# Decoding float64 weights with integer operations in a fused attention and two-FFN kernel

## The chip, the cores and the metric

The kernel runs on one core of one Trainium2 chip. The metric is the device time in microseconds (us) of one execution; the median of 3 runs of the kernel before is 885.85 us (885.5 to 887.36). A core has five engines with queues of their own: PE multiplies matrices, DVE, ACT and POOL work on elements, SP issues the DMAs.

## The reference

Windowed causal attention (4 batches, 8 heads, 576 positions, head size 64) gives 2304 tokens of 512 features. A first feed-forward block (512 to 1024 to 512, softmax gate and layer norm) and a second one (512 to 1536 to 512, SiLU gate) follow:

```python
def _attn_ref(q, k, v):
    scores = scale * np.matmul(q, k.transpose(0, 1, 3, 2))
    scores = np.where(mask, scores + bias[None], -1000000000.0)
    scores = scores - np.max(scores, axis=-1, keepdims=True)
    attn = np.exp(scores)
    attn = attn / (np.sum(attn, axis=-1, keepdims=True) + 1e-09)
    return np.matmul(attn, v).astype(np.float32)

def _moe_ref(x, w_in, w_out, g_ln):
    h = x @ w_in
    e = np.exp(h - np.max(h, axis=-1, keepdims=True))
    solu = h * (e / (np.sum(e, axis=-1, keepdims=True) + 1e-09))
    mu = np.mean(solu, axis=-1, keepdims=True)
    var = np.mean((solu - mu) ** 2, axis=-1, keepdims=True)
    return ((solu - mu) / np.sqrt(var + 1e-06) * g_ln @ w_out).astype(np.float32)

def _moe2_ref(x, w_gate, w_val, w_out):
    g = x @ w_gate
    return (g * (1.0 / (1.0 + np.exp(-g))) * (x @ w_val) @ w_out).astype(np.float32)
```

The five weight matrices arrive as float64. [...]

## The kernel before

The order of all instructions is made when the kernel is built. Generators describe the tasks, and an `Emitter` (its `run`, line 158) plays them against a model of engine times (`t_act`, `t_dve`, `t_pool`) and hands out instructions by a rank; where a step has several possible engines it takes the one that ends first by the model plus a handicap (1.6 us for DVE, 0.7 us for ACT). On the chip every engine then works through its own queue in that fixed order and waits on semaphores.

There are 20 attention steps (`score` and `attend`, lines 314 and 353: scores on PE, line 339; bias and row maximum on DVE, line 372; exponential on ACT, line 375; sum and reciprocal on DVE, lines 381 and 382; normalising on POOL, ACT or DVE, lines 387 and 389; transposes on PE, line 409; values on PE, line 441). Behind them come 18 token tiles of the first block (`up`, line 527; `flip`, line 589; `down1`, line 618), whose results go to DRAM (`yscr`) and come back (`load_y`, line 716). When attention has ended, its memory is given to the second block (`second_region`, line 666), which goes through 12 column chunks of the second weights, two to a pass (`load_w2`, line 701; `gate_val`, line 740; `down`, line 777). All large matrix products are in `pieces`, line 523. Each float32 operand is split into a rounded part (`high`, lines 202 and 203, on ACT or DVE) and a remainder (`low`, lines 206 and 208, on DVE or POOL), and three products are summed.

`decode` (line 213) makes one 128x512 block of weights, 52 times: 8 blocks of `w_in`, 8 of `w_out`, 36 of the second weights. A 512 KB DMA brings the pairs of words into tile `dw` (2 buffers). `lw` and `hw` are the low and the high words, every other element of `dw`. Before the change:

- line 225, ACT: `b` is the square of the high word read as float32.
- line 230, DVE: `a` is the high word, or zero where the square is under a limit.
- line 232, DVE: `b` is `a` shifted left by 3, masked. Line 234, DVE: the sign is put in from `a`.
- line 236, DVE: `a` is the exponent of `b`. Line 238, DVE: `a` becomes the low word scaled by that exponent. Buffer `dw` is given back here (line 240).
- line 241, POOL (or line 242, DVE): `b` is `b` plus `a` in float32.
- for `w_out` a scale on ACT or DVE (line 245), then `high` and `low`. `da` and `db` have 2 buffers each; `da` is held to the addition, `db` to the end of `low`.

All DMAs go through the one SP queue (line 193), in the order of the plan.

Of the kernel before, what the change touches and what calls it, by code (L numbers as in the profile page):

```python
# [8 lines left out]
F32 = mybir.dt.float32  # L9
F32R = mybir.dt.float32r  # L10
U32 = mybir.dt.uint32
AF = mybir.ActivationFunctionType
ALU = mybir.AluOpType
AX = mybir.AxisListType
# [7 lines left out]
P = 128  # L22
# [28 lines left out]
MIN_HIGH = 2.0 ** -15 * 1.125  # L51
# [123 lines left out]
def attention_then_two_ffns(ctx: ExitStack, tc: tile.TileContext, qk, v, w_in, w_out, g_ln, w2, ident_d, bias_d, out):  # L175


    nc = tc.nc
    em = Emitter()
    PE, DVE, ACT, POOL, DMA = "PE", "DVE", "ACT", "POOL", "DMA"  # L180
    yscr = nc.dram_tensor("yscr", [NT // 256, P, KM, 256], F32).ap()

    def t_act(n, sbuf=True, table=False):
        return (94 if sbuf else 51) + 94 * table + 0.833 * n

    def t_dve(n, fast=False):
        return 68 + (0.52 if fast else 1.042) * n

    def t_pool(n):
        return 149 + 2.104 * n  # L190

    def dma(dst, src, nbytes, deps=()):
        return (DMA, nbytes / 360.0, lambda: nc.sync.dma_start(dst, src), deps, 2000.0)

    const = ctx.enter_context(tc.tile_pool(name="const", bufs=1))
    dec = ctx.enter_context(tc.tile_pool(name="dec", bufs=1))
# [4 lines left out]
    def high(hi, src, n, sbuf=True):  # L201
        return [(ACT, t_act(n, sbuf), lambda: nc.scalar.copy(hi, src)),  # L202
                (DVE, t_dve(n, sbuf), lambda: nc.vector.tensor_copy(hi, src))]

    def low(lo, src, hi, n, sbuf=True):
        ways = [(DVE, t_dve(n), lambda: nc.vector.tensor_sub(lo, src, hi.bitcast(F32)))]
        if sbuf:
            ways.append((POOL, t_pool(n), lambda: nc.gpsimd.tensor_sub(lo, src, hi.bitcast(F32))))  # L208
        return ways

    dw_s, da_s, db_s = Slots(NDW), Slots(2), Slots(2)

    def decode(hi, lo, src, scale=None):


        yield dw_s
        words = dec.tile([P, 512, 2], U32, tag="dw", bufs=NDW, name="dw")
        got = yield dma(words, src.bitcast(U32), 524288)
        lw, hw = words[:, :, 0], words[:, :, 1]
        hf = hw.bitcast(F32)  # L220
        yield got
        yield db_s
        b = dec.tile([P, 512], U32, tag="db", bufs=2, name="db")
        bf = b.bitcast(F32)
        x = yield (ACT, t_act(512), lambda: nc.scalar.activation(bf, hf, AF.Square))  # L225
        yield x
        yield da_s
        a = dec.tile([P, 512], U32, tag="da", bufs=2, name="da")
        af = a.bitcast(F32)
        x = yield (DVE, t_dve(512), lambda: nc.vector.scalar_tensor_tensor(  # L230
            af, bf, MIN_HIGH * MIN_HIGH, hf, ALU.is_ge, ALU.mult), [x])
        x = yield (DVE, t_dve(512, True), lambda: nc.vector.tensor_scalar(  # L232
            b, a, 3, 0x3FFFFFF8, ALU.logical_shift_left, ALU.bitwise_and), [x])
        x = yield (DVE, t_dve(512), lambda: nc.vector.scalar_tensor_tensor(  # L234
            b, a, 0xC0000000, b, ALU.bitwise_and, ALU.bitwise_or), [x])
        x = yield (DVE, t_dve(512, True), lambda: nc.vector.tensor_scalar(  # L236
            a, b, 0xFF800000, None, ALU.bitwise_and), [x])
        x = yield (DVE, t_dve(512), lambda: nc.vector.scalar_tensor_tensor(  # L238
            af, lw, 2.0 ** -52, af, ALU.mult, ALU.mult), [x])
        em.give(dw_s, x)  # L240
        x = yield ([(POOL, t_pool(512), lambda: nc.gpsimd.tensor_add(bf, bf, af)),  # L241
                    (DVE, t_dve(512), lambda: nc.vector.tensor_add(bf, bf, af))], [x])
        em.give(da_s, x)
        if scale is not None:
            x = yield ([(ACT, 93 + t_act(512), lambda: nc.scalar.activation(bf, bf, AF.Copy, scale=scale)),
                        (DVE, 456, lambda: nc.vector.tensor_scalar_mul(bf, bf, scale))], [x])
        x = yield (high(hi, bf, 512), [x])
        x = yield (low(lo, bf, hi, 512), [x])
        em.give(db_s, x)
        yield x  # L250
# [102 lines left out]
    def attend(u):  # L353
# [17 lines left out]
        for j in range(2):  # L371
# [3 lines left out]
            ex.append((yield (ACT, t_act(cols, True, True), lambda j=j: nc.scalar.activation(  # L375
                e[0:n, j, 0:cols], e[0:n, j, 0:cols], AF.Exp, bias=st[0:n, j:j + 1], scale=-1.0,
                accum_out=st[0:n, 2 + j:3 + j]), [d])))
# [6 lines left out]
        def normalize(eng):  # L384
            if eng is nc.scalar:
                for j in range(2):
                    nc.scalar.activation(e[0:n, j, 0:cols], e[0:n, j, 0:cols], AF.Copy, scale=st[0:n, 6 + j:7 + j])
            else:
# [97 lines left out]
    def load_in():  # L486
        for half in range(2):
            cs = slice(half * 512, half * 512 + 512)
            for r in range(KM):
                def one(half=half, r=r, cs=cs):  # L490
                    yield from decode(win[0][:, r, cs], win[1][:, r, cs], w_in[r * P:(r + 1) * P, cs])
                d = em.start(one(), PW_IN + 0.01 * (half * KM + r))
                chain(d, win_ok[half][r])

    def load_out():
        for r in range(KF1):
            def one(r=r):
                if r == 0:
                    gln_ok.append((yield dma(gln, g_ln, 4096)))
                yield gln_ok[0]  # L500
                yield from decode(wout[0][:, r, :], wout[1][:, r, :], w_out[r * P:(r + 1) * P, :], gln[:, r:r + 1])
            d = em.start(one(), PW_OUT + 0.05 * r)
            chain(d, wout_ok[r])
# [23 lines left out]
    def up(i):  # L527
# [28 lines left out]
        for q, (a, a2) in enumerate(((sm, su), (sm2, su2))):  # L556
            y = yield (ACT, t_act(512, False, True), lambda q=q, a=a: nc.scalar.activation(
                e[:, q], h[q], AF.Exp, bias=mx, accum_out=a), [x])
            us.append((yield (DVE, t_dve(512), lambda q=q, a2=a2: nc.vector.scalar_tensor_tensor(
# [4 lines left out]
        for q, a in enumerate((va, va2)):  # L564
            vs.append((yield (ACT, t_act(512, True, True), lambda q=q, a=a: nc.scalar.activation(
                h[q], e[:, q], AF.Square, bias=nmu32, scale=1.0 / 32, accum_out=a), [x])))

# [133 lines left out]
    def load_w2(c):  # L701
        yield w2_s
        wp = pools["w2p"]
        t = [wp.tile([P, DF2], F32R, tag=f"w2{a}", bufs=NW2, name=f"w2{a}") for a in range(2)]
        wc[c] = t
        for j in range(3):
            cs = slice(j * 512, (j + 1) * 512)
            yield from decode(t[0][:, cs], t[1][:, cs], w2[c, :, cs])
            x = yield (POOL, 0.0, lambda: None)
            yield x  # L710
            w2_ok[c][j].settle(x.time)
# [144 lines left out]
```

## Time and profile before

| | us |
|---|---|
| median of 3 runs | 885.85 |
| the profiled execution | 887.44 |
| its span | 885.7 |
| PE busy | 825.1 (93%) |
| DVE busy | 492.9 (56%) |
| ACT busy | 372.8 (42%) |
| POOL busy | 317.0 (36%) |

The profile is of one execution, of 887.44 us, 1.6 us above the median; 1.74 us of it lie outside the span. PE is the busiest engine, but it isn't full everywhere: in the first sixth of the span and in a stretch around 380 us the other engines are fuller and PE idles. An average over the whole span hides that, so the views are read by stretches. The clock column is the clock that PE was granted, as a share of its upper level.

### The profile page before, as it was taken

How to read it: one execution, taken by the hardware profiler on the slowest of the kernel's cores; microseconds unless marked ns; L12 is line 12 of the kernel's file. 1: busy time of each engine (PE TensorE's matmuls, PEld its weight loads, DVE VectorE, ACT ScalarE, POOL GpSimd, SP SyncE). 2: the span in 40 equal slices, each digit the busy share in tenths (PEclk: the TensorE clock that was granted, in tenths of full speed). 3: DMA queues.
4: the chain of work that ended last, by engine and by line, in shares of the span. 5: the costliest groups of instructions: out<-in, count | busy, mean ns of one | idle time of the engine just before them, and what ended most of it. 6: DMA issues, size and time to landing. Idle time of an engine off the chain costs nothing.

```text
span 885.7 us, 13165 instructions
## 1 busy us (share of the span) xinstructions
PE 825.1 (93%) x4968; PEld 677.9 (77%) x4968; DVE 492.9 (56%) x1188; ACT 372.8 (42%) x948; POOL 317.0 (36%) x274
## 2 busy tenths in 40 slices
PE   5769879999999999968799999999999999999997
PEld 3547658788888888968588888887887887888885
DVE  5988993654556445888510186258337526822222
ACT  4667885864766656444432322122122213211110
POOL 2464661322123121665731154145216414521111
PEclk9779899999999999979999999999999999999999
DMA  7543311311121102333320022012003101100112
GB/s 253 168 138 105 96 60 44 107 37 54 50 72 49 36 8 97 119 104 112 120 94 1 1 72 72 1 49 72 24 0 86 58 1 48 47 1 13 60 57 85
DMA packets 23776, 59.12 MB, mean 67 GB/s; under 512 B 2592, under 2 KB 5280, under 8 KB 23712
## 3 DMA queue, kind: packets, MB, share of 16 engines
q1 hardware_dynamic: 23712, 58.28, 20.3%
q8 instruction: 39, 0.64, 0.3%
q14 instruction: 25, 0.20, 0.1%
HBM read 48.83 MB, written 9.44 MB: 66 GB/s over the span
## 4 chain that ended last, share of the span: by engine, by line
PE 70%; DVE 17%; POOL 4%; issue 4%; ACT 4%; DMA 1%; SPq 0%; POOLq 0%; ACTq 0%; DVEq 0%
PE gv L523 28%; PE bank L523 16%; PE o L523 15%; PE bank L441 3%; PE bank L409 3%; PE bank L339 3%; DVE db L234 2%; DVE da L230 2%; DVE da L238 2%; DVE da L236 2%; POOL db L241 2%; DVE e L372 2%; DVE db L232 1%; PE bank L605 1%; ACT e L375 1%
## 5 line engine op out<-in xcount | busy, mean ns | idle before, releaser
L523 PE MATMUL gv<-y,w 128*128 128x512 f32 (+1 forms) x1392 | 316.2, 378 | 3.1 <-POOL y L208 3.1
L523 PEld LDWEIGHTS gv<-y,w 128*128 128x128 f32 x1392 | 249.0, 189 | 57.6 <-POOL y L208 3.5
L523 PE MATMUL o<-w,a 128*128 128x512 f32 x648 | 170.0, 398 | 5.2 <-ACT ys L202 2.2
L208 POOL TENSOR_TENSOR a<-sg,a 128x512 fp32r<-128x512 f32 (+1 forms) x60 | 73.9, 1232 | 237.7 <-ACT a L202 237.2
L523 PEld LDWEIGHTS o<-w,a 128*128 128x128 f32 x648 | 121.1, 190 | 34.6 <-POOL a L208 3.8
L795 DVE TENSOR_TENSOR acc<-acc,o 128x512 f32<-128x512 f32 x90 | 61.2, 684 | 119.9 <-PE o L523 119.8
L523 PE MATMUL bank<-lnT,wout 128*128 128x256 f32 x864 | 116.9, 287 | 3.0 <-ACT lnT L202 2.5
L523 PEld LDWEIGHTS bank<-lnT,wout 128*128 128x128 f32 x864 | 109.0, 191 | 8.6 <-ACT lnT L202 2.7
L523 PE MATMUL bank<-win,xs 128*128 128x512 f32 x432 | 114.9, 404 | 0.1
L202 ACT CAST a<-sg 128x512 fp32r<-128x512 f32 (+1 forms) x59 | 34.0, 577 | 181.8 <-DVE sg L769 181.8
L769 DVE TENSOR_TENSOR sg<-sg,gv 128x512 f32<-128x512 f32 (+1 forms) x58 | 37.1, 639 | 126.7 <-PE gv L523 97.2
L241 POOL TENSOR_TENSOR db<-db,da 128x512 f32<-128x512 f32 x51 | 72.0, 1413 | 96.5 <-DVE da L238 93.9
L523 PEld LDWEIGHTS bank<-win,xs 128*128 128x128 f32 x432 | 76.5, 189 | 17.1 <-issue 2.1
L389 POOL TENSOR_TENSOR e<-e,st 128x512 f32<-128x512 f32 (+2 forms) x55 | 52.2, 948 | 103.9 <-DVE st L382 41.6
L375 ACT ACTIVATE e<-e,st 128x256 f32<-128x256 f32 (+2 forms) x160 | 75.0, 471 | 28.9 <-DVE st L372 28.8
L409 PE MATMUL bank<-ident,e 128*128 128x128 f32 (+2 forms) x288 | 47.7, 292 | 24.3 <-POOL e L389 15.0
L372 DVE CUSTOM_DVE_ANT_0 e<-bank,bias 128x256 f32<-128x256 f32 (+2 forms) x160 | 54.3, 376 | 17.2 <-PE bank L339 11.7
L409 PEld LDWEIGHTS bank<-ident,e 128*128 128x128 f32 (+2 forms) x288 | 31.4, 147 | 36.3 <-POOL e L389 18.2
L441 PE MATMUL bank<-pt,v 128*64 128x128 f32 (+2 forms) x576 | 51.4, 292 | 6.2 <-ACT pt L415 5.3
L230 DVE SCALAR_TENSOR_TENSOR da<-db,dw 128x512 f32<-128x512 f32 x52 | 46.6, 897 | 18.5 <-ACT db L225 18.4
L767 ACT ACTIVATE sg<-gv 128x512 f32<-128x512 f32 (+1 forms) x58 | 32.3, 557 | 56.3 <-PE gv L523 43.5
L202 ACT CAST w<-db 128x512 fp32r<-128x512 f32 x35 | 21.7, 621 | 80.1 <-POOL db L241 80.0
(70 smaller groups left out, 906.3 us busy)
## 6 DMA issues: line engine op xcount, KB each, us to landing
dw<-w SPq DMA_DIRECT2D x36, 512.0 KB, 3.6
raw<-qk SPq DMA_DIRECT2D x38, 256.0 KB, 3.7
yscr<-ys SPq DMA_DIRECT2D x9, 512.0 KB, 2.9
ysg<-yscr SPq DMA_DIRECT2D x9, 512.0 KB, 3.3
out<-acc SPq DMA_DIRECT2D x18, 256.0 KB, 2.0
v<-v SPq DMA_DIRECT2D x16, 256.0 KB, 2.8
dw<-w_in SPq DMA_DIRECT2D x8, 512.0 KB, 4.0
dw<-w_out SPq DMA_DIRECT2D x8, 512.0 KB, 3.5
```

The source lines that it names most:

```text
L202: return [(ACT, t_act(n, sbuf), lambda: nc.scalar.copy(hi, src)), (DVE, t_dve(n, sbuf), lambda: nc.vector.tensor_copy(hi, src))]
L208: ways.append((POOL, t_pool(n), lambda: nc.gpsimd.tensor_sub(lo, src, hi.bitcast(F32))))
L230: x = yield (DVE, t_dve(512), lambda: nc.vector.scalar_tensor_tensor(af, bf, MIN_HIGH * MIN_HIGH, hf, ALU.is_ge, ALU.mult), [x])
L241: x = yield ([(POOL, t_pool(512), lambda: nc.gpsimd.tensor_add(bf, bf, af)), (DVE, t_dve(512), lambda: nc.vector.tensor_add(bf, bf, af))], ...
L372: d = yield (DVE, t_dve(cols), lambda j=j: nc.vector.tensor_tensor_reduce(e[0:n, j, 0:cols], sc[0:n, j * 256:j * 256 + cols], bias[0:n, 2 ...
L375: ex.append((yield (ACT, t_act(cols, True, True), lambda j=j: nc.scalar.activation(e[0:n, j, 0:cols], e[0:n, j, 0:cols], AF.Exp, bias=st[0 ...
L389: eng.tensor_tensor(e[0:n, :, 0:cols], e[0:n, :, 0:cols], st[0:n, 6:8].unsqueeze(2).to_broadcast([n, 2, cols]), ALU.mult)
L409: nc.tensor.transpose(tp[0:kp, kb, j, 0:n], e[0:n, j, x * P:x * P + kp], ident[0:n, 0:n])
L441: nc.tensor.matmul(px[j * 64:(j + 1) * 64, pr, 0:n], vt[c - 1 + kb][0:kp, h * 64:(h + 1) * 64], pt[0:kp, kb, j, 0:n], start=(kb == 1), sto ...
L523: nc.tensor.matmul(o, terms[m][0], terms[m][1], start=(m == 0), stop=(m == len(terms) - 1))
L769: x = yield (DVE, t_dve(n), lambda: nc.vector.tensor_mul(sg, sg, gv[1][0]), [x, gv[1][1]])
L795: y = yield (DVE, t_dve(512), lambda o=o, tt=tt: nc.vector.tensor_add(acc[tt], acc[tt], o), [x])
```

## The change

`decode` is rewritten. The low word is read by ACT, scaled by 2^-29 and written as an int32 into `a` (a rounded 0 to 8). ACT takes the absolute value of the high word instead of its square. DVE clamps it from below, shifts it left by 3 with a mask, and puts in the sign bits straight from the high word in `dw`. `dw` is given back after that third DVE operation. POOL then adds `a` to the bit pattern of `b` as int32; the choice of DVE for this addition is gone. What follows (scale, `high`, `low`) stays. `a` is now taken before `b`.

```diff
     def decode(hi, lo, src, scale=None):
         yield dw_s
         words = dec.tile([P, 512, 2], U32, tag="dw", bufs=NDW, name="dw")
         got = yield dma(words, src.bitcast(U32), 524288)
         lw, hw = words[:, :, 0], words[:, :, 1]
         hf = hw.bitcast(F32)
         yield got
+        yield da_s
+        a = dec.tile([P, 512], U32, tag="da", bufs=2, name="da")
+        r = yield (ACT, t_act(512), lambda: nc.scalar.activation(a.bitcast(I32), lw, AF.Copy, scale=2.0 ** -29))
         yield db_s
         b = dec.tile([P, 512], U32, tag="db", bufs=2, name="db")
         bf = b.bitcast(F32)
-        x = yield (ACT, t_act(512), lambda: nc.scalar.activation(bf, hf, AF.Square))
-        yield x
-        yield da_s
-        a = dec.tile([P, 512], U32, tag="da", bufs=2, name="da")
-        af = a.bitcast(F32)
+        x = yield (ACT, t_act(512), lambda: nc.scalar.activation(bf, hf, AF.Abs))
+        x = yield (DVE, t_dve(512, True), lambda: nc.vector.tensor_scalar_max(bf, bf, MIN_HIGH), [x])
+        x = yield (DVE, t_dve(512, True), lambda: nc.vector.tensor_scalar(
+            b, b, 3, 0x3FFFFFF8, ALU.logical_shift_left, ALU.bitwise_and), [x])
         x = yield (DVE, t_dve(512), lambda: nc.vector.scalar_tensor_tensor(
-            af, bf, MIN_HIGH * MIN_HIGH, hf, ALU.is_ge, ALU.mult), [x])
-        x = yield (DVE, t_dve(512, True), lambda: nc.vector.tensor_scalar(
-            b, a, 3, 0x3FFFFFF8, ALU.logical_shift_left, ALU.bitwise_and), [x])
-        x = yield (DVE, t_dve(512), lambda: nc.vector.scalar_tensor_tensor(
-            b, a, 0xC0000000, b, ALU.bitwise_and, ALU.bitwise_or), [x])
-        x = yield (DVE, t_dve(512, True), lambda: nc.vector.tensor_scalar(
-            a, b, 0xFF800000, None, ALU.bitwise_and), [x])
-        x = yield (DVE, t_dve(512), lambda: nc.vector.scalar_tensor_tensor(
-            af, lw, 2.0 ** -52, af, ALU.mult, ALU.mult), [x])
+            b, hw, 0xC0000000, b, ALU.bitwise_and, ALU.bitwise_or), [x])
         em.give(dw_s, x)
-        x = yield ([(POOL, t_pool(512), lambda: nc.gpsimd.tensor_add(bf, bf, af)),
-                    (DVE, t_dve(512), lambda: nc.vector.tensor_add(bf, bf, af))], [x])
+        x = yield (POOL, t_pool(512), lambda: nc.gpsimd.tensor_tensor(
+            b.bitcast(I32), b.bitcast(I32), a.bitcast(I32), ALU.add), [x, r])
         em.give(da_s, x)
```

## Rows read from the trace of the kernel before

**Rows 1.** Stretches: PE, PEld, DVE, ACT, POOL busy us (instructions), clock, DMA share, GB/s.
```profile
22.00:132.00 110.00, 84.96 (x596) 63.19 (x597) 104.74 (x297) 82.99 (x235) 59.89 (x53) 0.86 0.36 114
...
180.00:336.00 156.00, 156.00 (x1293) 132.00 (x1293) 81.35 (x320) 94.66 (x284) 37.88 (x45) 1.00 0.13 44
336.00:440.00 104.00, 87.45 (x602) 78.58 (x601) 79.35 (x151) 50.56 (x111) 58.68 (x43) 0.93 0.36 117
440.00:865.00 425.00, 423.88 (x1935) 346.54 (x1934) 185.38 (x262) 100.76 (x178) 139.88 (x107) 1.00 0.13 40
```
**Rows 2.** PE's groups, 22 to 132 us: busy us, mean ns | idle before, releasers.
```profile
L409 PE MATMUL bank<-ident,e 128*128 128x128 f32 (+2 forms) x92 | 18.3, 330 | 23.4 <-POOL e L389 14.2 <-DVE st L372 4.0 <-DVE lnT L206 3.1
```
**Rows 3.** DVE's groups, 22 to 132 us, same columns.
```profile
L230 DVE SCALAR_TENSOR_TENSOR da<-db,dw 128x512 f32<-128x512 f32 x14 | 14.7, 1059 | 0.0
L234 DVE SCALAR_TENSOR_TENSOR db<-da,db 128x512 uint32<-128x512 uint32 x14 | 12.3, 878 | 0.0
L238 DVE SCALAR_TENSOR_TENSOR da<-dw,da 128x512 f32<-128x512 uint32 x14 | 11.0, 789 | 0.0
L236 DVE TENSOR_SCALAR da<-db 128x512 uint32<-128x512 uint32 x14 | 7.8, 557 | 0.0
L232 DVE TENSOR_SCALAR db<-da 128x512 uint32<-128x512 uint32 x14 | 6.2, 448 | 0.0
```
**Rows 4.** Durations min/median/max ns of the decode's instructions, 22 to 132 us.
```profile
L230 DVE SCALAR_TENSOR_TENSOR da<-db,dw x14: 677/1064/1740, 25.0 to 120.5; 128x512 f32<-128x512 f32 x14
L232 DVE TENSOR_SCALAR db<-da x14: 404/413/901, 25.9 to 122.2; 128x512 uint32<-128x512 uint32 x14
L234 DVE SCALAR_TENSOR_TENSOR db<-da,db x14: 668/678/1768, 26.5 to 123.0; 128x512 uint32<-128x512 uint32 x14
```
**Rows 5.** ACT's groups, 22 to 132 us, columns as in rows 2.
```profile
L225 ACT ACTIVATE db<-dw 128x512 f32<-128x512 f32 x14 | 9.2, 663 | 0.0
L387 ACT ACTIVATE e<-e,st 128x256 f32<-128x256 f32 (+2 forms) x20 | 8.5, 475 | 5.0 <-DVE st L382 4.8
L245 ACT ACTIVATE db<-db,gln 128x512 f32<-128x512 f32 x8 | 5.8, 725 | 4.7 <-POOL db L241 4.7
L202 ACT CAST win<-db 128x512 fp32r<-128x512 f32 x7 | 4.3, 610 | 4.9 <-POOL db L241 4.9
```
**Rows 6.** POOL's groups, 22 to 132 us, columns as in rows 2.
```profile
L241 POOL TENSOR_TENSOR db<-db,da 128x512 f32<-128x512 f32 x13 | 18.3, 1409 | 23.3 <-DVE da L238 20.6 <-DVE st L381 2.7
L582 POOL TENSOR_SCALAR e<-e,mst 128x512 f32<-128x512 f32 x8 | 7.1, 896 | 0.2
```
**Rows 7.** SP's queue from 351 us: start, us, what.
```profile
351.15 6.26 SPq L193 DMA_DIRECT2D ysg<-yscr  x2
361.31 16.76 SPq L193 DMA_DIRECT2D dw<-w  x4
```
**Rows 8.** DVE from 355 us, columns as in rows 7, [idle before <-releaser].
```profile
360.59 0.69 DVE L238 SCALAR_TENSOR_TENSOR da<-dw,da 128x512 f32<-128x512 uint32 x1
...
366.95 1.40 DVE L232 TENSOR_SCALAR db<-da 128x512 uint32<-128x512 uint32 x1
```
**Rows 9.** POOL, 361 to 387 us.
```profile
361.36 1.29 POOL L241 TENSOR_TENSOR db<-db,da 128x512 f32<-128x512 f32 x1 [4.29 <-DVE da L238]
...
366.34 1.72 POOL L241 TENSOR_TENSOR db<-db,da 128x512 f32<-128x512 f32 x1
...
382.49 1.65 POOL L241 TENSOR_TENSOR db<-db,da 128x512 f32<-128x512 f32 x1 [1.09 <-DVE da L238]
384.86 1.26 POOL L208 TENSOR_TENSOR w<-db,w 128x512 fp32r<-128x512 f32 x1 [0.73 <-ACT w L202]
```
**Rows 10.** PE, 375 to 391 us.
```profile
375.26 1.68 PE L523 MATMUL bank<-y,w 128*128 128x256 f32 x12
...
386.18 4.21 PE L523 MATMUL bank<-y,w 128*128 128x256 f32 x18 [8.36 <-POOL w L208]
```
**Rows 11.** DMA issues, whole span: KB each, median us from issue to landing.
```profile
dw<-w SPq DMA_DIRECT2D x36, 512.0 KB, 3.6
```
**Rows 12.** ACT's table loads, whole span, columns as in rows 2.
```profile
L375 ACT ACT_TABLE_LOAD x1 | 1.3, 1283 | 0.7 <-PEq L849 0.7
L767 ACT ACT_TABLE_LOAD x1 | 1.3, 1283 | 0.0
```

More of the change, by code (lines that the diff above doesn't have):

```diff
@@ L11 @@
 U32 = mybir.dt.uint32
+I32 = mybir.dt.int32
 AF = mybir.ActivationFunctionType
```

## The prediction

> **What bounds the kernel now.** I first read the busy shares by stretch [rows 1]. From 180 to 336 us PE is busy for all 156.00 us, and from 440 to 865 us for 423.88 of 425: there PE sets the time, and an edit to other engines is worth nothing. Two stretches are different. From 22 to 132 us (stage A, where the 16 blocks of the first weights are decoded beside attention) PE is busy 84.96 of 110 us, at a granted clock of 0.86, while DVE is busy 104.74 us, 95%. From 336 to 440 us (stage B, the change to the second block, with its first 12 decodes) PE is busy 87.45 of 104 us at 0.93. So the time that an edit of `decode` can give back is PE's idle time in these two, 25.0 and 16.6 us, and some clock.
>
> Next I asked who holds PE up. In stage A nearly all its idle time, 23.4 us, stands before the transposes of attention, released by POOL's normalising and by DVE [rows 2]; these are late because DVE's queue is full. The five DVE instructions of a decode show no idle time before them in stage A [rows 3]: they never wait for data, data wait for them. In stage B the one large stall is 8.36 us before 386.18 us, released by POOL's remainder of a weight block [rows 10].
>
> **The DVE part of the change.** Per decode, DVE now does 1.059 + 0.448 + 0.878 + 0.557 + 0.789 = 3.73 us [rows 3]. The change leaves three instructions. The shift is line 232 as it was. The clamp is an operation of the same kind (one tile, one constant): the trace has no float32 one of this size alone, and I bound it by line 232 (0.45) and line 236 (0.56). The sign keeps the form of line 234, with one input now read from `dw` at every other element as line 230 reads it: 0.88 to 1.06. I take 0.45 + 0.56 + 0.88 = 1.89 us, as the two nearest rows are of the same operations. The lower end is what they cost undisturbed, 0.41 + 0.41 + 0.68 = 1.50 [rows 4]; the upper end 0.56 + 0.56 + 1.06 = 2.18. In stage A, 14 decodes fall inside the 110 us, so DVE loses 14 x (3.73 - 1.89) = 25.8 us (21.7 to 31.2) and falls from 104.7 to 79 us.
>
> Why the same instruction costs 0.41 or 1.40 us is seen in one place: line 232 at 366.95 lasts 1.40 us [rows 8] and ends just after POOL's addition, which runs from 366.34 to 368.06 [rows 9]. DVE instructions stand still while POOL works. The Trainium skill, GPSIMD Engine Reference, section Key points, says that POOL shares its SBUF interfaces with DVE and collides with two-port modes and with two SBUF inputs; that would leave all three new DVE instructions exposed, and by it the upper end would be the better guess. It would make the sum about 2 us smaller, inside the range.
>
> **The ACT part.** Absolute value takes the place of the square, both one pass over the same strided words: no difference. The rounding of the low word is new. No row has an int32 output; the nearest are the strided square, 0.663, and the dense cast, 0.610 [rows 5], so I take 0.66 (bounds 0.56 to 0.71, the distance of those two to either side). In stage A that is 14 x 0.66 = 9.2 us on top of 82.99: ACT becomes the fullest engine with 92 of 110 us. In stage B it is 8 us on top of 50.56 of 104, and later 24 more on 100.76 of 425: no cost there.
>
> The new instruction stands first in the decode and waits for a buffer `da`, which POOL's earlier addition gives back; behind it in ACT's queue stand exponentials and casts. ACT already waits so before the scale and the cast, 4.7 and 4.9 us in stage A, for POOL's addition [rows 5]. That addition in turn waited for DVE, 20.6 us [rows 6], so I expect the wait to shrink with DVE's load and book it at nothing. If it stays, it is the second rival below.
>
> **The POOL part.** One addition for one addition. No POOL instruction here works on int32; its float32 forms took 1.409 us for two inputs and 0.896 for one [rows 6]. I take 1.41. Below, 0.90 would change nothing, since POOL is idle for 50 of stage A's 110 us. Above there is no row; what would follow is the third rival.
>
> **Buffers and the SP queue.** `dw` is given back after ACT's two and DVE's three instructions instead of ACT's one and DVE's five. In stage B that shows: the third weight DMA issues at 361.31 [rows 7], directly after line 238 of the first decode ends at 361.28 [rows 8], though SP had finished the two loads in front of it at 351.15 + 6.26 = 357.41. With three DVE instructions the buffer is free before 357.4, so this DMA goes 3.9 us earlier. No DMA is added or moved past another.
>
> **What stage B gives.** PE's stall ends when the fifth decode's remainder is done, 384.86 + 1.26 = 386.12 [rows 9, 10]. Additions one to five end from 362.65 to 384.14: 5.4 us a decode. After the change the pair of `dw` buffers allows one per (3.6 [rows 11] + 1.33 + 1.89) / 2 = 3.4 us, and POOL needs 1.41 + 1.3 = 2.7 plus its share of token tiles. An estimate of 4.2 us a decode, with the first addition ending near 358.5, puts the fifth at 375.3 and its remainder at 377.5, before PE comes to need it: PE is through with the products at 375.26 (and a few transposes) some 8.4 us ahead of 386.18. So the stall goes, 8.4 us, and with it the slow start after it (18 products in 4.21 us where 12 took 1.68, so 1.7 us) [rows 10]. What is late next are some 8 us of short waits for the last token tiles in this stage, which can grow when PE arrives earlier. I book 8 of the 10 us, with 3 and 12 as ends.
>
> **What stage A gives.** ACT at 92 us is now the longest. If it ran as full as DVE did, 95%, the stage would last 97 us, 13 us less. If the plan moved part of ACT's optional work to DVE, both would hold (92 + 79) / 2 = 86, and at 95% the stage would last 90 us, 20 us less. If ACT filled only 87%, it would be 106, 4 us less. I take 13, nearest to what the fullest engine of this stage does now. Elsewhere: nothing, PE is full.
>
> **Sum.** 13 + 8 = 21 us. 887.4 - 21 = 866.4 for an execution like the profiled one; 885.85 - 21 = 865 for the median.
>
> **The rivals.**
>
> 1. ACT inherits the bound and keeps part of its own waits (stage A gives 4, stage B 5): 877 us. For it: ACT at 92 of 110 with long chains through POOL. Against it: ACT's waits in stage A lead to DVE, directly or through POOL's addition [rows 5, 6].
> 2. ACT's queue blocks as before. ACT is idle 27.0 us in stage A. If all of that stays, the stage lasts 92 + 27 = 119 us, 9 us longer, and stage B's 8 us only balance it: 887 us. It decides from an idle time above 110 - 92 = 18 us on.
> 3. POOL's int32 addition is slow. POOL has 50.1 us free in stage A, 3.6 a decode; past 1.41 + 3.6 = 5.0 us per addition POOL is the bound of the stage. At 6 us POOL would need 59.9 + 14 x 4.6 = 124 us in stage A (14 lost) and 58.7 + 12 x 4.6 = 114 in stage B (10 lost): 910 us, slower. The trace has no row for or against. The Trainium skill, GPSIMD Engine Reference, section Engine selection, says that the cores add 32-bit integers natively; no run here shows it. By that the addition would cost what it costs now.
> 4. Absolute value isn't in the loaded table. The trace has two table loads of 1.283 us in all [rows 12]; copy, square and exponential alternate without one. If each absolute value needed a load, and the next exponential another, ACT would get 14 x 2.57 = 36 us more in stage A, 128 us for 110, and the kernel would lose about 18 - 5 = 13 us: 899 us. The Trainium skill, ScalarE: Activation LUTs, section Table sets: the hidden batching unit, has absolute value in every set; the rows agree for copy and square, and none shows the absolute value.
> 5. Everything falls in place: PE's 25 us in stage A go, with some 4 us of clock, and 10 in stage B: 847 us. For it: PE's waits there all lead to DVE. Against it: ACT at 84%.
>
> A part that doesn't do what it says (the clamp at 0.88 instead of 0.56) would cost 14 x 0.3 = 4.5 us on a DVE that is no longer the bound: inside the range.
>
> **How the numbers follow.** Forecast (stage A 8 to 18, stage B 4 to 11: 857 to 873) 0.55; rival 1, 0.17; rival 2, 0.07; rival 3, 0.05; rival 4, 0.03; rival 5, 0.13. The predicted time is 865. The lower end is rival 5's, 847; the upper one takes in rival 1 and stops short of rival 2: 884. Differences under 0.2% (1.8 us) a measurement of this kernel can't tell from none. Faster: 0.55 + 0.17 + 0.13 and a little of rival 2 = 0.87; same 0.04, slower 0.09.
>
> **What would show it.** Right: DVE under 80% busy in the first 120 us with decode instructions that now wait for data; the transposes' 23 us before PE shrunk by half; no stall of several us before PE's first products with the second weights; no third table load; POOL's int32 addition near 1.4 us; PE busy time a few us under 825, from the clock. Wrong: ACT over 95% busy in stage A or idle behind POOL; the 8.4 us stall back in another place, such as the last token tiles; and above all stretches after 440 us in which PE is no longer full.

## The result, and the profile after

The changed kernel takes 862.62 us (median; 862.19 to 863.66), beside 885.89 us for the kernel before in the same comparison: a ratio of 0.9741, 95% interval 0.9728 to 0.9754. That is 23.3 us less. The profiled execution took 862.31 us, 25.1 us less than the one before (887.44); all that is read from traces below is read from these two, so some 2 us of it are their distance from the medians.

The page of the changed kernel, busy time of each engine (share of the span, instructions) and PE's clock by 40 slices:

```profile
span 860.5 us, 13066 instructions
...
PE 819.9 (95%) x4968; PEld 674.7 (78%) x4968; DVE 427.9 (50%) x1097; ACT 394.9 (46%) x991; POOL 296.6 (34%) x267
...
PEclk9789999999999999998999999999999999999999
```

The span is 25.2 us shorter. PE has the same 4968 products, is busy 5.2 us less (825.1 before) and idle 40.6 us where it was idle 60.6. DVE lost 65 us, ACT gained 22.

To see where, I cut both traces at the same event, the first DMA of the second weights (343.41 us before, 326.40 after). Up to there PE has issued the same 2446 products in both. The columns are those of rows 1; first the kernel before, then the changed one:

```profile
0.00:343.40 343.40, 306.07 (x2446) 248.17 (x2446) 228.31 (x799) 227.19 (x681) 119.41 (x128) 0.96 0.25 82
```
```profile
0.00:326.40 326.40, 303.15 (x2446) 244.57 (x2446) 207.20 (x771) 229.53 (x688) 119.39 (x130) 0.97 0.27 87
...
22.00:113.00 91.00, 80.69 (x589) 59.14 (x589) 81.57 (x261) 79.98 (x228) 57.85 (x52) 0.90 0.42 141
...
320.00:430.00 110.00, 98.24 (x644) 88.17 (x641) 66.88 (x125) 60.80 (x129) 55.85 (x44) 0.94 0.39 129
430.00:840.00 410.00, 410.00 (x1879) 336.50 (x1878) 152.33 (x217) 109.24 (x196) 121.67 (x96) 1.00 0.12 36
```

So the first part is 17.0 us shorter: 14.1 us of PE's idle time and 2.9 us of its busy time, at a clock of 0.97 for 0.96. The other 8.2 us come behind it. The decoding of the first weights, which took up to 133 us, now ends at 113 us. In the 91 us from 22 to 113 DVE, ACT and PE are busy 90%, 88% and 89%: nobody is full, and three engines are level, where DVE alone was at 95% [rows 1]. After 430 us PE is full as before.

The decode's groups in the first 135 us of the changed kernel (columns as in rows 2), which answer to rows 3:

```profile
L234 DVE SCALAR_TENSOR_TENSOR db<-dw,db 128x512 uint32<-128x512 uint32 x16 | 14.9, 930 | 0.2
L231 DVE TENSOR_SCALAR db<-db 128x512 f32<-128x512 f32 x16 | 10.2, 640 | 2.0 <-ACT db L230 1.8
L232 DVE TENSOR_SCALAR db<-db 128x512 uint32<-128x512 uint32 x16 | 9.9, 618 | 0.1
```

They sum to 2.19 us a decode. And over the whole span, the int32 operations and the table loads:

```profile
L237 POOL TENSOR_TENSOR db<-db,da 128x512 int32<-128x512 int32 x52 | 69.7, 1340 | 71.8 <-DVE db L234 55.3 <-ACT sg L763 3.5 <-ACT pt L411 3.1
L226 ACT ACTIVATE da<-dw 128x512 int32<-128x512 uint32 x52 | 34.8, 669 | 7.5 <-DMA dw<-w 6.4 <-DMA dw<-w_in 0.7 <-DMA dw<-w_out 0.2
...
L371 ACT ACT_TABLE_LOAD x1 | 1.3, 1283 | 0.7 <-PEq L845 0.7
L763 ACT ACT_TABLE_LOAD x1 | 1.3, 1283 | 0.0
```

The int32 addition costs what the float32 one did (1.34 us; 1.41 in rows 6, for stage A), the int32 output on ACT costs nothing extra, and absolute value needed no further table.

The change of blocks, on POOL and PE of the changed kernel (columns as in rows 7 and 8):

```profile
341.65 1.30 POOL L237 TENSOR_TENSOR db<-db,da 128x512 int32<-128x512 int32 x1 [1.83 <-ACT e L553]
...
357.99 1.29 POOL L237 TENSOR_TENSOR db<-db,da 128x512 int32<-128x512 int32 x1 [2.23 <-DVE mst L570]
359.24 1.00 POOL L575 TENSOR_TENSOR mst<-mst,mhalf 128x1 f32<-128x1 f32 x1
360.34 1.68 POOL L578 TENSOR_SCALAR e<-e,mst 128x512 f32<-128x512 f32 x2
361.99 1.43 POOL L209 TENSOR_TENSOR w<-db,w 128x512 fp32r<-128x512 f32 x1
```
```profile
358.25 1.68 PE L519 MATMUL bank<-y,w 128*128 128x256 f32 x12
363.47 1.65 PE L519 MATMUL bank<-y,w 128*128 128x256 f32 x6 [3.54 <-POOL w L209]
...
382.72 1.91 PE L601 MATMUL bank<-ident,e 128*128 128x128 f32 x16
...
392.08 10.11 PE L519 MATMUL bank<-lnT,wout 128*128 128x256 f32 x68 [7.45 <-ACT lnT L203]
```

Additions one to five end from 342.95 to 359.28 us, 4.1 us apart instead of 5.4 [rows 9]. The stall of 8.36 us [rows 10] is down to 3.54, because token work (lines 575 and 578) stands in POOL's queue between the fifth addition and its remainder. But 7.45 us of idle time have come up at another place, before the products of the last tokens, where 2.5 us stood in the kernel before:

```profile
408.33 1.23 PE L523 MATMUL bank<-lnT,wout 128*128 128x256 f32 x8 [2.49 <-ACT lnT L202]
```

### The profile page after: what moved, and what is told of

The parts are those of the page before. It is cut to its first block, busy times and chain, and to the rows that moved or that the text cites. A ratio compares the mean times of both kernels' runs of the same rounds, so it can differ in the third digit from the quotient of the medians.

```text
span 860.5 us, 13066 instructions
## 1 busy us (share of the span) xinstructions
PE 819.9 (95%) x4968; PEld 674.7 (78%) x4968; DVE 427.9 (50%) x1097; ACT 394.9 (46%) x991; POOL 296.6 (34%) x267
## 4 chain that ended last, share of the span: by engine, by line
PE 77%; DVE 8%; ACT 7%; DMA 2%; issue 2%; POOL 2%; SPq 0%; POOLq 0%; DVEq 0%; ACTq 0%
PE gv L519 34%; PE o L519 17%; PE bank L519 16%; PE bank L437 3%; PE bank L335 3%; PE bank L405 3%; ACT e L371 2%; DVE db L234 1%; DVE db L231 1%; PE bank L601 1%; DVE db L232 1%; DVE e L368 1%; POOL db L237 1%; DVE e L555 1%; ACT db L230 1%
## 5 line engine op out<-in xcount | busy, mean ns | idle before, releaser
L519 PE MATMUL o<-w,a 128*128 128x512 f32 x648 | 167.9, 395 | 2.6 <-ACT a L203 1.3
L209 POOL TENSOR_TENSOR a<-sg,a 128x512 fp32r<-128x512 f32 (+1 forms) x53 | 65.1, 1227 | 245.6 <-ACT a L203 245.5
L519 PE MATMUL bank<-win,xs 128*128 128x512 f32 x432 | 117.6, 408 | 1.4 <-DVE xs L207 0.7
L237 POOL TENSOR_TENSOR db<-db,da 128x512 int32<-128x512 int32 x52 | 69.7, 1340 | 71.8 <-DVE db L234 55.3
L335 PE MATMUL bank<-raw,raw 64*128 64x128 f32 (+2 forms) x576 | 45.2, 299 | 7.9 <-DMA raw<-qk 7.8
L234 DVE SCALAR_TENSOR_TENSOR db<-dw,db 128x512 uint32<-128x512 uint32 x52 | 51.3, 987 | 1.1
```

The source lines that it names most:

```text
L237: x = yield (POOL, t_pool(512), lambda: nc.gpsimd.tensor_tensor(b.bitcast(I32), b.bitcast(I32), a.bitcast(I32), ALU.add), [x, r])
L335: nc.tensor.matmul(banks[ks[r]][0:n, o:o + w], raw[c][0][rows, 2 * qd + j, 0:n], raw[c - 1 + kb][1][rows, 2 * qd + j, 0:w], start=True, st ...
L519: nc.tensor.matmul(o, terms[m][0], terms[m][1], start=(m == 0), stop=(m == len(terms) - 1))
```

## The experiments

All kernels below are variants of the changed one. Medians differ a little between comparisons, so the ratio to the kernel before is given with each. "First part" is the time to the first DMA of the second weights and "rest" what follows it, both in the profiled execution, which lies up to 3 us off the median (low_old). "DVE per decode" is the sum of the mean durations, in the first 140 us, of the DVE instructions that every decode has; a step that the plan gave to DVE only in some decodes isn't in it.

| kernel | DVE per decode, us | first part, us | rest of the span, us | median, us | ratio to before |
|---|---|---|---|---|---|
| before | 3.70 | 343.4 | 542.3 | 885.9 | 1 |
| after | 2.19 | 326.4 | 534.1 | 862.6 | 0.9741 |
| dve_load | 3.68 | 345.9 | 571.1 | 918.0 | 1.0375 |
| dve_load_planned | 3.65 | 344.4 | 542.9 | 889.5 | 1.0053 |
| low_old | 3.58 | 341.5 | 544.3 | 884.6 | 0.9993 |
| old_test | 2.47 | 335.2 | 534.7 | 873.7 | 0.9875 |
| old_test_plan | 2.53 | 329.3 | 537.3 | 868.3 | 0.981 |
| other_plan | 2.14 | 335.8 | 535.0 | 871.4 | 0.9843 |
| pool_load | 2.38 | 332.2 | 542.2 | 876.1 | 0.9903 |
| act_load | 2.07 | 329.0 | 536.7 | 867.9 | 0.9809 |
| buf_db3 | 2.14 | 332.9 | 530.9 | 865.7 | 0.9789 |
| bias_dve | 2.03 | 336.8 | 536.9 | 874.7 | 0.9886 |
| bias_up | 2.28 | 330.9 | 533.7 | 868.5 | 0.9821 |
| w2_high_only | 2.22 | 327.0 | 529.0 | 857.3 | 0.9685 |

**dve_load: DVE's load put back.**

```diff
-        x = yield (DVE, t_dve(512), lambda: nc.vector.scalar_tensor_tensor(
-            b, hw, 0xC0000000, b, ALU.bitwise_and, ALU.bitwise_or), [x])
+        def sign():
+            nc.vector.scalar_tensor_tensor(b, hw, 0xC0000000, b, ALU.bitwise_and, ALU.bitwise_or)
+            nc.vector.tensor_scalar(b, b, 0xFFFFFFF8, None, ALU.bitwise_and)
+            nc.vector.scalar_tensor_tensor(b, hw, 0xC0000000, b, ALU.bitwise_and, ALU.bitwise_or)
+
+        x = yield (DVE, t_dve(512), sign, [x])
```

> The changed kernel with two more DVE instructions in each decode, in the same place of the queue (a mask and the sign instruction once more; they change nothing in the values). The plan doesn't know of them, so all other queues keep the order of the changed kernel. DVE does five instructions per decode again, as before the change. Theory (DVE's load in the decode stretches is what the change took away): DVE gets back 0.6 + 0.9 = 1.5 us per decode, 21 us in the first 113 us, where it is busy 90%; the kernel goes back to 880 to 892 us. Rival (the gain came from the new order of the plan, not from DVE's load): 862 to 870 us.

Measured: 918.0 us, ratio 1.0375 (1.0357 to 1.0393). The sign of the effect is the theory's, its size is off: 33 us more than before the change, beyond both expectations. In the first part the order of the changed kernel with the old load gives the old picture again [rows 1]: 345.9 us in all, DVE busy 103.61 of 110 us, PE 86.38. The surplus is in the rest: 22 us of PE idle time at the change of blocks (16.6 before), 14 us where PE had always been full, and 10 us more of busy time, at a clock of 0.98 behind 490 us where it had been 1.00 [rows 1]:

```profile
22.00:132.00 110.00, 86.38 (x587) 62.84 (x588) 103.61 (x293) 82.26 (x229) 57.82 (x53) 0.82 0.35 121
...
490.00:897.00 407.00, 392.82 (x1768) 318.58 (x1767) 179.07 (x262) 101.74 (x182) 115.93 (x92) 0.98 0.11 36
```

PE's waits from 490 to 897 us (us in total, times, longest):

```profile
PE o L523 <- DVE a L207: 8.3, 4, 2.1
PE o L523 <- ACT a L203: 4.7, 4, 1.3
```

Products of the second block wait for activations whose remainder stands in DVE's queue behind decodes that are longer than the plan assumed.

**dve_load_planned: the same, with a plan that knows it.**

```diff
-        x = yield (DVE, t_dve(512), sign, [x])
+        x = yield (DVE, 2 * t_dve(512) + t_dve(512, True), sign, [x])
```

> As dve_load, but the plan is told of the two added DVE instructions and orders all queues with them in mind. dve_load took 918 us, 33 us more than before the change. Theory (DVE's load is the cause in both stretches, and the surplus over before comes from a plan that knew nothing of it, above all the 14 us of PE idle time after 490 us): 884 to 898 us, and PE full again after the change of blocks. Rival (ACT's extra pass together with DVE's load makes the decode itself slower than before): 905 to 918 us.

Measured: 889.5 us, ratio 1.0053 (1.0037 to 1.007), as the theory had it, and PE is busy 413.8 of 415 us again from 450 to 865. Of the 55 us that dve_load lost against the changed kernel, 28 are thus the plan's ignorance of the load, and 27 the load with an order made for it. This kernel does DVE's five instructions, ACT's two and the int32 addition, and is 0.5% slower than before the change.

**low_old: half of the change.**

```diff
+        x = yield (DVE, t_dve(512, True), lambda: nc.vector.tensor_scalar(
+            a, b, 0xFF800000, None, ALU.bitwise_and), [x])
+        x = yield (DVE, t_dve(512), lambda: nc.vector.scalar_tensor_tensor(
+            af, lw, 2.0 ** -52, af, ALU.mult, ALU.mult), [x])
         em.give(dw_s, x)
-        x = yield (POOL, t_pool(512), lambda: nc.gpsimd.tensor_tensor(
-            b.bitcast(I32), b.bitcast(I32), a.bitcast(I32), ALU.add), [x, r])
+        x = yield ([(POOL, t_pool(512), lambda: nc.gpsimd.tensor_add(bf, bf, af)),
+                    (DVE, t_dve(512), lambda: nc.vector.tensor_add(bf, bf, af))], [x])
```

(The cut is shortened: the rounding on ACT is taken out, and `a` is taken behind the absolute value, as before the change.)

> One half of the change alone: absolute value, clamp and sign as changed (no comparison with two inputs), but the low word as before (exponent and scaling on DVE, two instructions; float32 addition on POOL or DVE; no rounding on ACT). DVE does five instructions, 0.60 + 0.65 + 0.92 + 0.56 + 0.79 = 3.5 us per decode against 3.73 before and 2.17 after. Theory (DVE's time per decode decides): 876 to 886 us. Rival (the clamp, which old_test showed to be worth 11 us, brings that here too by shortening the chain): 870 to 876 us.

Measured: 884.6 us, ratio 0.9993 (0.9981 to 1.0006): no change. Absolute value, clamp and the sign from the high word bring nothing while DVE still does five instructions. dve_load_planned has all the new operations, five instructions on DVE, and gains nothing either. So together the two point at the number of DVE's instructions and not at one of the new operations. low_old alone can't show it, as its order is another too.

**old_test, old_test_plan and other_plan: load and plan apart.** old_test replaces only the clamp by the old comparison:

```diff
-        x = yield (ACT, t_act(512), lambda: nc.scalar.activation(bf, hf, AF.Abs))
-        x = yield (DVE, t_dve(512, True), lambda: nc.vector.tensor_scalar_max(bf, bf, MIN_HIGH), [x])
+        x = yield (ACT, t_act(512), lambda: nc.scalar.activation(bf, hf, AF.Square))
+        x = yield (DVE, t_dve(512), lambda: nc.vector.scalar_tensor_tensor(
+            bf, bf, MIN_HIGH * MIN_HIGH, hf, ALU.is_ge, ALU.mult), [x])
```

> The changed kernel with the old treatment of small values: square on ACT, and on DVE the comparison with both inputs in place of the clamp, everything else as changed. DVE pays 0.9 to 1.06 us in place of 0.60 per decode, 4 to 6 us in the first 113 us. Theory (DVE's load counts): 864 to 870 us. Rival (the rounding of the low word on ACT and the int32 addition carry the whole gain, the clamp nothing): 862 to 863 us.

Measured: 873.7 us, ratio 0.9875 (0.9859 to 0.9892): 11 us for some 0.3 us of DVE time per decode, more than either expectation. With 28 decodes in the stretches that count (16 of the first weights and 12 at the change of blocks), 0.3 us is 8 us of DVE time in all. So I separated the instructions from the order that came with them. old_test_plan has old_test's instructions with the clamp's cost told to the plan (`t_dve(512, True)`), other_plan the changed kernel's instructions with the comparison's cost told (`t_dve(512)`).

> The instructions of old_test (square and comparison in place of absolute value and clamp), in the order of the changed kernel: the plan is told that the comparison costs what the clamp costs, and all queues keep the changed kernel's order. old_test took 11 us more than the changed kernel for some 0.3 to 0.44 us more DVE time per decode. Theory (DVE's load carries the difference): 868 to 875 us. Rival (the plan that goes with it carries most of it): 863 to 867 us.

> The instructions of the changed kernel in the order of old_test: the plan is told that the clamp costs what the comparison costs. Theory (DVE's load carries the difference of 11 us): 862 to 866 us. Rival (the plan carries it): 868 to 874 us.

Measured: 868.3 us, ratio 0.981 (0.9795 to 0.9824), and 871.4 us, ratio 0.9843 (0.9824 to 0.9862). In the order of the changed kernel the comparison costs 0.9810 - 0.9741 = 0.7%, 6 us; in the other order 0.9875 - 0.9843 = 0.3%, 3 us, which is hardly clear of noise: the intervals of old_test and other_plan overlap by a hair. Changing only the order costs 1.0%, 9 us, with the new instructions and 0.65%, 6 us, with the old ones. So more of old_test's 11 us comes from the order than from the load. old_test_plan lies just inside the theory's range, other_plan in the rival's.

**act_load and pool_load: the price of the other two engines.** Both keep the order of the changed kernel.

```diff
+            nc.scalar.activation(a.bitcast(I32), lw, AF.Copy, scale=2.0 ** -29)
             nc.scalar.activation(a.bitcast(I32), lw, AF.Copy, scale=2.0 ** -29)
```
```diff
             nc.gpsimd.tensor_tensor(b.bitcast(I32), b.bitcast(I32), a.bitcast(I32), ALU.add)
+            nc.gpsimd.tensor_tensor(a.bitcast(I32), a.bitcast(I32), a.bitcast(I32), ALU.add)
```

> The changed kernel with the rounding of the low word done twice on ACT, plan and order unchanged. Theory (after the change DVE, ACT and PE are level at 88 to 90% of the first 113 us, so each counts): ACT gets 14 x 0.67 = 9 us more there and the kernel takes 866 to 876 us. Rival (DVE still sets the time and ACT's work lies beside it): 862 to 864 us.

> The changed kernel with a second int32 addition on POOL after the first in each decode (of a buffer that is given up behind it), plan and order unchanged. Theory (POOL isn't full, 64% in the first 113 us, but it holds up DVE's instructions and the remainders behind it): 866 to 880 us, and DVE's mean durations in the decode grow by 0.1 to 0.3 us each. Rival (POOL has 33 us to spare, so nothing happens): 862 to 864 us.

Measured: 867.9 us, ratio 0.9809 (0.9794 to 0.9824), and 876.1 us, ratio 0.9903 (0.9885 to 0.9922). Both rivals are out. 28 x 0.67 = 19 us more on ACT cost 6 us. 28 x 1.09 = 30 us more on POOL cost 14 us, though POOL was busy only 64%. One reason is seen in pool_load's DVE rows of the first 135 us:

```profile
L234 DVE SCALAR_TENSOR_TENSOR db<-dw,db 128x512 uint32<-128x512 uint32 x16 | 14.4, 900 | 0.2
L232 DVE TENSOR_SCALAR db<-db 128x512 uint32<-128x512 uint32 x16 | 11.8, 740 | 0.1
L231 DVE TENSOR_SCALAR db<-db 128x512 f32<-128x512 f32 x16 | 11.8, 739 | 1.8 <-ACT db L230 1.8
```

Clamp and shift, themselves untouched, went from 0.64 and 0.62 to 0.74 us; the sign, expected to grow too, did not. That is 0.19 us a decode, 3 us for the 16 of the first weights. That the remainder, which stands behind the second addition in POOL's queue, makes up the other part is argued from the order and not measured.

**buf_db3, bias_dve and bias_up: other settings.** Three buffers for `da` and `db` instead of two; the plan's handicap for DVE at 0.8 and at 2.4 us instead of 1.6:

```diff
-    dw_s, da_s, db_s = Slots(NDW), Slots(2), Slots(2)
+    dw_s, da_s, db_s = Slots(NDW), Slots(3), Slots(3)
```
```diff
-B_DVE = 1600.0
+B_DVE = 800.0
```

(The first cut is shortened: both tiles get `bufs=3`. bias_up has 2400.0 in the same line.)

> The changed kernel with three buffers each of da and db in place of two. Theory (the decode is limited by the engines' work, which three level engines share): 860 to 865 us. Rival (ACT and POOL wait for buffers that come back late, so that a third one takes their waits away): 850 to 858 us.

> The changed kernel with the plan's handicap for DVE halved (0.8 us for 1.6), so that DVE, which has less to do now, takes more of the work that ACT or POOL could also do. Theory (three engines are level at 88 to 90% in the first 113 us, so moving work among them gains nothing): 861 to 868 us. Rival (ACT is the bound and DVE has room): 850 to 860 us.

> The changed kernel with the plan's handicap for DVE at 2.4 us for 1.6: the optional work goes rather to ACT and POOL. Theory (three engines level): 861 to 870 us. Rival (DVE, which POOL holds up, is still the dearest engine in these stretches, and sparing it pays): 852 to 860 us.

Measured: 865.7 us, ratio 0.9789 (0.9774 to 0.9804); 874.7 us, 0.9886 (0.9871 to 0.9901); 868.5 us, 0.9821 (0.9805 to 0.9837). None of these beats the changed kernel, and no rival that looked for room on an engine was right. buf_db3 ended 0.7 us above the theory's range, bias_up inside it. bias_dve missed both expectations with 12 us more; in its trace PE waits 6.5 us for normalising on DVE and 4.9 us for token tiles on DVE, and the first part takes 336.8 us. All three settings give the plan another order too, which alone was worth 6 to 9 us above. So buf_db3's 3 us and bias_up's 6 us say nothing of the buffer or of the engines by themselves.

**w2_high_only: the new wait.**

```diff
-            yield from decode(t[0][:, cs], t[1][:, cs], w2[c, :, cs])
+            yield from decode(t[0][:, cs], t[1][:, cs], w2[c, :, cs], None, False)
```

(The cut is shortened: with False, `decode` leaves out the rounding and the addition.)

> The changed kernel without the low word in the 36 blocks of the second weights: no rounding on ACT and no addition on POOL there; the second weights are then cut to their high words. Theory (the 7.5 us before PE's products at 392 us are ACT's queue, where the casts of the last tokens stand behind decodes that wait for POOL's addition): PE's idle time in the change of blocks, 11.8 us, falls to 6 or less, and the kernel takes 853 to 859 us. Rival (the wait is the chain of the last token tiles themselves): it stays at 9 to 12 us, 860 to 864 us.

Measured: 857.3 us, ratio 0.9685 (0.967 to 0.9699). PE's idle time in the change of blocks (310 to 410 us here) is 7.4 us instead of 11.8, and the wait before the products of the last tokens 2.6 us instead of 7.5. Where the changed kernel waited 3.5 us for POOL's remainder, 4.1 us now go by, released by a token tile on DVE. The time is in the theory's range, the idle time between the two expectations. But this kernel has an order of its own too, and 5 us in all is less than an order alone can move, so the total doesn't tell the theory from the order. ACT's queue in the changed kernel shows how much of the wait it can explain:

```profile
382.59 0.68 ACT L226 ACTIVATE da<-dw 128x512 int32<-128x512 uint32 x1
383.17 0.68 ACT L230 ACTIVATE db<-dw 128x512 f32<-128x512 f32 x1
383.88 0.69 ACT L226 ACTIVATE da<-dw 128x512 int32<-128x512 uint32 x1
384.48 0.67 ACT L230 ACTIVATE db<-dw 128x512 f32<-128x512 f32 x1
387.22 0.62 ACT L203 CAST w<-db 128x512 fp32r<-128x512 f32 x1 [2.08 <-POOL db L237]
387.75 0.58 ACT L203 COPY ys<-bank 128x512 f32<-128x512 f32 x1
388.22 1.08 ACT L203 CAST lnT<-bank 128x512 fp32r<-128x512 f32 x2
```

PE's transposes end at 384.63; the cast of their result starts at 388.22, behind two decodes' passes and a cast that waits 2.08 us for POOL. A second pair of casts follows at 391.47, again behind a decode. Without the low word part of that goes, but a cast that waits for the sign on DVE stays. So the new wait has the decode in ACT's queue as a part, by the queue's order; how much is the chain of the last tokens themselves stays open.

## Why the prediction was right

21 us were booked, and 23.3 came by the medians. What bounds the kernel and where PE's idle time would come back were right. DVE's price was mis-sized, the clock was left out of the sum, and the step that makes ACT the bound of stage A failed; the sum hardly shows it.

**What bounds the kernel.** Right. dve_load_planned and low_old put DVE's load back in two ways, and both end within 5 us of the kernel before, with the first part at 344.4 and 341.5 us (343.4 before); dve_load, with the order of the changed kernel, has 345.9. The 14 us of PE's idle time that the first part gave up are from the 25 us that rows 1 and 2 pointed at: the idle time before the transposes is 9.8 us between 22 and 132 us, from 23.4. A rival that no run sets apart is the length of a decode's chain, which grows with each instruction put back. In stage A the rows speak for the load: nearly all of PE's idle time there stands before attention's transposes and waits for no decoded block [rows 2], and before the change the decode's instructions found DVE's queue full [rows 3]. At the change of blocks, where DVE was busy 79 of 104 us [rows 1], it stays open which of the two counts.

**DVE's price.** Mis-sized, and at its upper end: 2.19 us a decode where 1.89 was taken (1.50 to 2.18 given). The clamp took 0.64 and the shift 0.62, both above the 0.56 that was allowed for, the sign 0.93. Over the whole span (min/median/max in ns):

```profile
L231 DVE TENSOR_SCALAR db<-db x52: 405/427/2256, 13.0 to 739.1; 128x512 f32<-128x512 f32 x52
L232 DVE TENSOR_SCALAR db<-db x52: 407/428/1531, 13.5 to 739.5; 128x512 uint32<-128x512 uint32 x52
L234 DVE SCALAR_TENSOR_TENSOR db<-dw,db x52: 672/693/1787, 14.0 to 741.5; 128x512 uint32<-128x512 uint32 x52
```

The prediction told from one case that DVE stands still while POOL works, and the traces bear out that POOL is the cause. Of the changed kernel's 156 decode instructions on DVE, 66 ran with no POOL instruction beside them, and none of these took over 0.01 us more than the median of its kind; the 61 that took over 0.05 us more all ran beside one. So it is in the other 13 traces. The rule is too strong, though, as 29 ran beside POOL and paid less than that. What the price left out is that POOL's work gets denser as the stage gets shorter: POOL was busy 54% of stage A [rows 1] and 64% of the 91 us after. In the first 140 us a decode instruction shared 0.33 us with POOL and lost 0.16 us by it before the change; after it, 0.42 and 0.22 us; in pool_load, with more POOL work in the same order, 0.57 and 0.28. (POOL's spans in a profile are rough, so these are estimates.) The sentence from the Trainium skill, GPSIMD Engine Reference, section Key points, on shared SBUF interfaces pointed to the upper end, and the trace agrees: medians of 427 and 428 ns for clamp and shift over the whole span, means of 625 and 738. (That the upper end makes the sum about 2 us smaller has no working: by the prediction's own rule ACT's 92 us set stage A at either price.)

**ACT's price and the bound after.** The pass was priced at 0.66 and took 0.67 us. That ACT would be the fullest engine was wrong: DVE, ACT and PE came out level (81.57, 79.98 and 80.69 of 91 us). act_load confirms that ACT counts, at about a third of each added microsecond.

**Stage A: 13 us booked, 17.0 measured in the first part.** 14.1 us are idle time and 2.9 us busy time at a higher clock. The 13 was worked out from ACT at 92 us as the bound, and that step failed. What came is near the other branch of the prediction, in which the plan takes work off ACT and the stage lasts 90 us: it lasted 91. Over the span ACT gained only 22.1 us, though the new pass alone takes 34.8. That 13 lies so near the idle time gained is therefore in part luck. The clock has no term in the sum; the prediction has it as "some clock", in rival 5 and among its signs.

**Stage B: 8 booked, 8.2 measured in all that lies behind the first DMA** (6.0 us idle, 2.2 busy). The steps, though, are a sum of errors that cancel. The third weight DMA came 15.2 us after the first, predicted 14.0, before 17.9. The pitch of the additions was 4.1 us, predicted 4.2. The stall should have gone whole, and 3.5 us stayed. The margin was thin: 375.26, from which the prediction takes PE to be through, is where its twelve products start [rows 10], and PE came to need the remainder at 386.18 - 8.36 = 377.8, only 0.3 us behind the 377.5 forecast for it. Token work of 2.7 us, for which the step from the fifth addition to its remainder had no room, was more than that. The idle time came back at the last tokens with 7.5 us, named as what would be late next; and 2 us came from busy time at a higher clock.

**The signs.** The transposes' wait, the table loads, the addition and PE's busy time came as the prediction wrote them, and PE stayed full behind 430 us. Three did not: DVE was busy 82% of the first 120 us, not under 80%; its decode instructions waited 2.3 us in all for data in the first 135 us, so it is still their queue that they wait for; and two stalls of several us are left, 3.5 us before products with the second weights and 7.5 at the last tokens, one of the signs of being wrong.

**The rivals.** ACT inheriting the bound, 877 us: no, and in stage A it was idle 11.0 us where 27.0 had been. ACT's queue blocking as before: seen once, at the last tokens, and not in stage A, where ACT's waits before scale and cast fell from 9.6 to 1.6 us. Int32 on POOL slow: out, 1.34 us. Another table for the absolute value: out, two loads as before. Of the Trainium skill's two sentences, the one on absolute value in every set (ScalarE: Activation LUTs, Table sets) agrees with the two loads. The one on the native integer addition (GPSIMD Engine Reference, Engine selection) gives no price; that int32 costs what float32 costs is what the rows show. Everything in place, 847 us: not reached.

**What the prediction did not ask.** How much of the gain belongs to the order that the plan happened to find. Five orders or settings for the same decode instructions (after, buf_db3, bias_up, other_plan, bias_dve) give 862.6, 865.7, 868.5, 871.4 and 874.7 us; their mean is 868.6. Three kernels with some 3.6 us or more of DVE time per decode (before, low_old, dve_load_planned) give 885.9, 884.6 and 889.5, mean 886.7. The two groups don't overlap. By the means, about 18 of the 23 us belong to DVE's lighter load, and about 5 to an order that is the best of the five tried. The settings weren't varied for the kernel before, so that split is rough.

## What to carry to other kernels

Where an engine is full in one stage, count what an edit takes from that engine in that stage alone, and then ask which engine is next: here DVE's busy time in the first part fell by 21 us and the part by 17, and two other engines were then level with it. A variant built by a planner changes load and order at once; telling the plan the old cost, and the old instructions the new plan, separates the two, and here the order alone was worth 6 to 9 us. Where two variants differ in their order too, a difference smaller than that says nothing of the load. And an engine that isn't full can still be dear: POOL lengthened DVE's instructions, the more so the shorter the stage became.

## What the runs showed of the hardware

An int32 addition of two 128x512 tiles on POOL took 1.34 us, as much as the float32 one; with both inputs the same tile it took 1.09 us. On ACT a uint32 input read at every other element with int32 output took 0.669 us, as the float32 pass over the same words (0.663). DVE's clamp of 128x512 took between 0.405 and 2.256 us, with a median of 0.427. In all 14 traces DVE's decode instructions took over 0.05 us more than undisturbed only where a POOL instruction ran beside them; with none beside them they took at most 0.02 us more than their median. A POOL that is busy 64% of the first weights' stage still cost nearly half a microsecond of kernel time for each added one.
